# A list scheduler that counts VectorE's time twice where an operation may choose its engine, and durations of products fitted to the trace

## The chip, the cores and the metric

The kernel runs on one core of a Trainium2 chip. The metric is the device time of one execution in microseconds. Before the change it is 1055.45 us (median of 3 runs, 1055.14 to 1056.12).

A core has five engines with a queue of instructions each: PE (TensorE, the matrix products, with PEld for its weight loads), DVE (VectorE), ACT (ScalarE), POOL (GpSimd) and SP (SyncE, which here issues nearly all DMAs). An engine works its queue in order. Between engines there are only semaphores.

## The reference

Three layers follow one another, all in fp32:

```python
# attention: 4 batches, 8 heads, 576 positions of 64, blocks of 64 causal
scores = q @ k.T / 8, masked to block_i >= block_j
attn   = exp(scores - max); attn /= sum + 1e-9
x      = attn @ v                       # 2304 tokens x 512
# first MLP, 512 -> 2048 -> 512, softplus
h = x @ w_in;  g = max(h, 0) + log1p(exp(-|h|));  x = g @ w_out
# second MLP, 512 -> 1536 -> 512, after RMS norm
xn = x / sqrt(mean(x*x) + 1e-6) * rms_g
g = xn @ w_gate;  out = (g * sigmoid(g) * (xn @ w_val)) @ w_out
```

## The kernel before

**Products in two halves.** A fp32 product is made of three passes over operands split into a high and a low part: high x high, high x low, low x high (`PASSES`). So before each product somebody has to make the two parts: a cast (or a scaled copy) writes the high part, a subtraction the low part. For the weights this is `w_unit` (lines 437 to 464): a 128 x 512 piece `wraw` is loaded, ScalarE (L448, L449), VectorE (L458, L452, L456) and GpSimd (L461, an integer addition) make the value `wa`, then the cast `w<-wa` (L327 on ScalarE or L328 on VectorE) and the difference (L337 on VectorE or L338 on GpSimd) fill the two parts of `w`. 68 such pieces pass in the first 660 us.

**Attention.** Work goes by units of one batch, one third of the queries and one pair of heads, 48 in all, and by three query tiles in a unit. For each tile PE makes the scores, VectorE takes their maximum (L627), ScalarE their exponential with its sum (L661), VectorE the reciprocal (L669, L670). Then the rows are scaled by it. The first 12 units (`whole(u)`) take plain fp32 products: the scores `P` are scaled in place (`s_turn`, L703 GpSimd, L704 VectorE or L705 ScalarE), PE transposes them against `ones` (L716), a copy brings them back (`pt`, L722 or L723), and PE multiplies by v. The other 36 units write a high part `pst` in fp16 (`s_split`, L681 GpSimd, L682 VectorE or L683 ScalarE), VectorE the low part (L686), and a DMA transposes both (`pt<-pst`, L693).

**First MLP.** Six blocks of 384 tokens. Its first 9 of 16 slices of the hidden layer (`g1`, products `x,w`; `g2`, products `g,w`) run while attention goes on: each block follows the units that it needs, so that PE always has some wide products to put between the small ones of attention. The other 7 slices follow from some 380 us on, with the weights of the second MLP being prepared beside them.

**Second MLP.** From 660 us to the end PE alone is busy, with nothing left to prepare.

**Who sets the order.** Nothing of this is in program order. Every operation is first entered in a `Plan` with an engine, a duration, a key (roughly its due time) and what it reads and writes. `Plan.schedule` then runs a model of the engines and picks, engine by engine, the ready operation with the lowest key. An operation with `alt` has two or three engines to choose from: in `arrive` it takes the one on which it would end first, by the time at which that engine is free, the durations of the ready operations ahead of it there, and its own duration times `WEIGHT` (line 74). `Plan.emit` repeats this 12 times with keys moved towards the latest start times, keeps the order with the earliest modelled end, and writes the instructions in that order. PE's model has a clock: it runs at half speed unless the tick before it held enough columns (`cols`). Durations come from small functions: `t_mm` for one pass of a product of n columns, `t_mm16` for the columns themselves. `t_mm` also sets the keys of the MLP steps (`step`, `step2`).

Of the kernel before, what the change touches and what calls it, by code (L numbers as in the profile page):

```python
# [68 lines left out]
class Plan:  # L69
# [1 line left out]


    TICK = 10.24 / 3
    WEIGHT = {"ACT": 1, "DVE": 1, "POOL": 1}
    LAT = {"PE": 0.2, "ACT": 0.14, "DVE": 0.2, "POOL": 0.08, "SP": 0.0}
    LAT_DVE = {"DVE": 0.13, "POOL": 0.25}

# [67 lines left out]
    def schedule(self, key):  # L145
# [12 lines left out]
        def arrive(i):  # L158
            if i in self.alts:
                best = None  # L160
                for c, (e, d, _) in enumerate(self.alts[i]):
                    ahead = sum(took[k] for x, k in ready[e] if x < key[i])
                    t = max(ready_at[i], free[e] + ahead)
                    if self.on_port(i, e):
                        t = max(t, port_free)
                    t += d * self.WEIGHT[e]
                    if best is None or t < best[0]:
# [126 lines left out]


def t_mm(n):
    return max(0.11, (n + 32) / 2400)


def t_mm16(n):  # L300
    return n * 0.4167e-3
# [42 lines left out]
def kernel(  # L344
# [14 lines left out]
    S = kT.shape[3]  # L359
# [9 lines left out]
    NG = 3  # L369
    GQ = 192  # L370
# [103 lines left out]
    vhl = [kp.tile([128, 2, KT, 128], FP16, name=f"vhl{p}") for p in range(NP)]  # L474
# [17 lines left out]
    def aop(*args, **kw):  # L492
        att_ops.append(op(*args, **kw))

    def whole(u):
        return u < 12
# [13 lines left out]
    v_pst = [R_pst.new() for _ in range(NP // 2)]  # L510
    v0 = lambda p: v_pst[p // 2]().rearrange("p j c -> p (j c)").bitcast(FP32)[:, 640 * (p % 2):640 * (p % 2) + 640].rearrange("p (a c) -> p a c", c=128)

    def q_slot(u):
        i = u % (4 if whole(u) else 2)
        if i < 2:
            return ("qf", i), lambda: qf[i]
        t = v_pst[i - 2]
        return (t, "q"), lambda: t().rearrange("p j c -> p (j c)").bitcast(FP32)[:, 1280:1664].rearrange("p (i c) -> p i c", i=NG)
# [64 lines left out]
    def ring_a(u):  # L583
        return R_a0 if u * NG < len(units) * NG // NB else R_a
# [9 lines left out]
    def s_tile(u, ib, key, after):  # L594
        b, g, p = units[u]
        n = 64 * (NG * g + ib + 1)
        chunks = [(0, n)] if n <= 512 else [(0, n // 2), (n // 2, n // 2)]
        d = qbd[u % 2]
        if ib == 0:
            pts[u], part[u] = R_pt.new(), (R_nm.new(), [])  # L600
            if not whole(u):
                psts[u] = R_pst.new()
        nm, done = part[u]
        qr = [("qbd", u % 2, l) for l in range(2)]
        kr = [("khl", p, 0), ("khl", p, 1)]
        if whole(u):
            kt, k = k_cell(p), lambda: k0(p)
            (qc, qt), kr = q_slot(u), [kt]
            qr = [qc]
        bank = []  # L610
        for c0, cn in chunks:
            sp = ring_a(u).new()
            bank.append(sp)

            def qk(sp=sp, c0=c0, cn=cn):
                if whole(u):
                    mm(sp()[:, :cn], qt()[:, ib, :], k()[:, c0:c0 + cn], True, True)
                    return
                for m, (a, c) in enumerate(PASSES):
                    mm(sp()[:, :cn], d[:, a, ib, :], khl[p][:, c, c0:c0 + cn], m == 0, m == 2)  # L620

            if c0 == 0:
                qk_op.append(len(plan.ops))
            aop("PE", max(0.213, 0.006 + cn * 1.667e-3) if whole(u) else 3 * t_mm(cn), key, qk, qr + kr, [sp], after=after, cols=t_mm16((2 if whole(u) else 3) * cn))
        for c, (sp, (c0, cn)) in enumerate(zip(bank, chunks)):
            col = ib + c
            aop("DVE", t_dve(cn), key, lambda sp=sp, col=col, cn=cn: nc.vector.tensor_reduce(nm()[:, col:col + 1], sp()[:, :cn], axis=AX.X, op=ALU.max, negate=True), [sp], [(nm, ib)])  # L627
        if len(chunks) == 2:
            aop("DVE", 0.07, key, lambda: nc.vector.tensor_tensor(nm()[:, ib:ib + 1], nm()[:, ib:ib + 1], nm()[:, ib + 1:ib + 2], ALU.min), [(nm, ib)], [(nm, ib)])
        done.append((ib, n, bank, chunks, key))  # L630
        if whole(u):
            if 0:
                if ib < NG - 1:
                    return
                todo, i0, i1 = done, 0, NG
            else:
                todo, i0, i1 = [done[-1]], ib, ib + 1
            cells = [(nm, i) for i in range(i0, i1)]
            small(("DVE", "POOL"), lambda e: e.tensor_scalar(nm()[:, i0:i1], nm()[:, i0:i1], 0.125, 1.0, ALU.mult, ALU.mult), key, cells, cells)
        else:  # L640
            todo = [done[-1]]
        for x in todo:
            s_exp(u, *x)
        if not 0:
            for x in todo:
                s_norm(u, x[0], x[0] + 1, x[4])
                (s_turn if whole(u) else s_split)(u, x[0], x[1], x[4])
        elif ib == NG - 1:
            s_norm(u, 0, NG, key)
            for x in done:  # L650
                s_split(u, x[0], x[1], x[4])
# [75 lines left out]
    def pv_whole(u, key):  # L727
        b, g, p = units[u]
        pt, o, pitch = pts.pop(u), ring_a(u).new(), 2 + g
        nj = (64 * (NG * g + NG) + 127) // 128  # L730
        pf = lambda: pt().rearrange("p j c -> p (j c)").bitcast(FP32).rearrange("p (x c) -> p x c", c=128)

        def prod():
            for j in range(nj):
                i0 = max(0, 2 * j - NG * g)
                kk = min(128, S - 128 * j)
                for h in range(2):
                    mm(
                        o()[64 * h:64 * h + 64, 64 * i0:GQ],
                        v0(p)[0:kk, j, 64 * h:64 * h + 64],  # L740
                        pf()[0:kk, slice(i0 * pitch + j, (NG - 1) * pitch + j + 1, pitch), 64 * h:64 * h + 64],
                        j == 0,
                        j == nj - 1,
                    )

        n = sum(GQ - 64 * max(0, 2 * j - NG * g) for j in range(nj))
        aop("PE", 2e-3 * n, key, prod, [(pt, i) for i in range(NG)] + [(v_pst[p // 2], p)], [o], cols=t_mm16(2 * n))
        jb, off = divmod(b * S + g * GQ, BLK)
        if jb not in x_b:
            x_b[jb] = R_x.new()  # L750
        x = x_b[jb]
        aop("ACT", t_act(GQ, False), key, lambda: nc.scalar.copy(x()[:, p, 0, off:off + GQ], o()[:, :GQ]), [o], [(x, p, 0)])
        aop("DVE", 0.27, key, lambda: nc.vector.tensor_tensor(x()[:, p, 1, off:off + GQ], o()[:, :GQ], x()[:, p, 0, off:off + GQ].bitcast(FP32), ALU.subtract), [o, (x, p, 0)], [(x, p, 1)])  # L753

    def pv(u, key):
        if whole(u):
            pv_whole(u, key)
            return
        b, g, p = units[u]
        pt, o = pts.pop(u), ring_a(u).new()  # L760
        njm = (64 * (NG * g + NG) + 127) // 128

        def prod():
            for j in range(njm):
                i0 = max(0, 2 * j - NG * g)
                kk = min(128, S - 128 * j)
                for m, (a, c) in enumerate(PASSES):
                    for h in range(2):
                        mm(
                            o()[64 * h:64 * h + 64, 64 * i0:GQ],  # L770
                            vhl[p][0:kk, a, j, 64 * h:64 * h + 64],
                            pt()[0:kk, slice(i0 * PITCH[g] + 2 * j + c, (NG - 1) * PITCH[g] + 2 * j + c + 1, PITCH[g]), 64 * h:64 * h + 64],
                            j == 0 and m == 0,
                            j == njm - 1 and m == 2,
                        )

        aop("PE", sum(3 * (t_mm16(GQ - 64 * max(0, 2 * j - NG * g)) + 0.027) for j in range(njm)), key, prod, [(pt, i) for i in range(NG)] + [("vhl", p, 0), ("vhl", p, 1)], [o], cols=sum(t_mm16(3 * (GQ - 64 * max(0, 2 * j - NG * g))) * min(128, S - 128 * j) / 128 for j in range(njm)))
        jb, off = divmod(b * S + g * GQ, BLK)
        if jb not in x_b:
            x_b[jb] = R_x.new()  # L780
        x = x_b[jb]
        aop("ACT", 0.304, key, lambda: nc.scalar.activation(x()[:, p, 0, off:off + GQ], o()[:, :GQ], ACTF.Copy, scale=dsc[p]), [o, ("dsc", p)], [(x, p, 0)])
        aop("DVE", 0.329, key, lambda: nc.vector.scalar_tensor_tensor(x()[:, p, 1, off:off + GQ], o()[:, :GQ], dsc[p], x()[:, p, 0, off:off + GQ].bitcast(FP32), ALU.mult, ALU.subtract), [o, ("dsc", p), (x, p, 0)], [(x, p, 1)])
# [235 lines left out]
    for s in range(len(steps) + LAG):  # L1019
# [5 lines left out]
        if s >= LAG:  # L1025
            j, f = steps[s - LAG]
# [5 lines left out]
        if s < len(steps) and steps[s][1] == NJ[steps[s][0]] - 1:  # L1032
            j = steps[s][0]
# [33 lines left out]
    for s in range(max(n_b + LAG, place[-1] + 1)):  # L1067
# [3 lines left out]
        if s < n_b:  # L1071
            j, f = steps[s]
            n = order.index(j)
# [3 lines left out]
        if LAG <= s < n_b + LAG:  # L1077
            j, f = steps[s - LAG]
            g2(j, f, f == NJ[j], f == NF1 - 1, key_b(s) + 0.5 * step)
            if f == NF1 - 1:  # L1080
                evac_b(j, key_b(s) + 0.6 * step)
                n = order.index(j) + 1
# [10 lines left out]
    for s in range(len(steps) + LAG):  # L1093
        key = t_2 + s * step2
# [4 lines left out]
        if s >= LAG:  # L1099
            j, f = steps[s - LAG]  # L1100
# [70 lines left out]
```

## Time and profile before

| | |
|---|---|
| median of 3 runs | 1055.45 us |
| the profiled execution | 1055.07 us |
| its span, first to last instruction | 1053.0 us |
| granted clock of TensorE, mean over the span | 0.992 |
| PE busy | 1015.6 us (96% of the span) |
| DVE busy | 710.2 us (67%) |
| ACT busy | 529.4 us (50%) |
| POOL busy | 163.9 us (16%) |
| chain that ended last | PE 56%, DVE 4%, DMA 3%, ACT 1% |

The averages hide that the span has different parts. In the page's 40 slices PE is busy for six to nine tenths in the first seven slices and for nine tenths or more from there to the end but for the last; VectorE is at nine tenths or near it over the first 14 slices and at two to four tenths in the last 15. A share of the whole span says little about any of them, so the rows below are taken stage by stage.

### The profile page before, as it was taken

What the parts mean: (1) busy time and instruction counts of PE and PEld (TensorE: products, weight loads), DVE (VectorE), ACT (ScalarE), POOL (GpSimd) and SP (SyncE); (2) the same over time, 40 slices, a digit from 0 to 9 for tenths busy, and PEclk for the clock granted to TensorE, in tenths of its full rate; (3) what the DMA queues carried; (4) which work ended last, traced back from release to release, by engine and by line L of the source; (5) the groups of instructions that cost most, each with busy time, mean ns of one, the idle gap of its engine ahead of it and who ended that gap; (6) DMA issues with size and microseconds to landing.
All of it is one profiled execution on the core that took longest, in us unless ns stands there. A gap on an engine that the chain in (4) does not pass through costs nothing.

```text
span 1053.0 us, 16902 instructions
## 1 busy us (share of the span) xinstructions
PE 1015.6 (96%) x6136; PEld 944.8 (90%) x6136; DVE 710.2 (67%) x1763; ACT 529.4 (50%) x1245; POOL 163.9 (16%) x225
## 2 busy tenths in 40 slices
PE   6798799999999999999999999999999999999998
PEld 4486689899999999999999999999999999999997
DVE  7989999999989967788879999522422422322222
ACT  6786787685767656777767563211211211211211
POOL 2333211211131003322333333000000000000000
PEclk8999899999999999999999999999999999999999
DMA  7444595785856453654544544300100100000000
GB/s 255 141 165 138 169 220 113 172 220 110 204 133 138 89 116 105 214 192 169 216 165 161 187 136 130 98 1 1 60 1 2 61 1 1 31 1 1 31 1 31
DMA packets 111635, 115.19 MB, mean 109 GB/s; under 512 B 84544, under 2 KB 92352, under 8 KB 110528
## 3 DMA queue, kind: packets, MB, share of 16 engines
q1 hardware_dynamic: 110976, 107.83, 36.3%
q0 software_dynamic: 576, 6.29, 1.6%
q8 instruction: 48, 0.79, 0.3%
q14 instruction: 35, 0.29, 0.1%
HBM read 72.03 MB, written 21.63 MB: 89 GB/s over the span
## 4 chain that ended last, share of the span: by engine, by line
PE 56%; DVE 4%; DMA 3%; ACT 1%; issue 1%; POOL 0%; ACTq 0%; DVEq 0%; POOLq 0%; SPq 0%
PE b L422 56%; DMA pt<-pst 1%; DMA wraw<-in_w2gv_dram 1%; DMA wraw<-in_w_dram 1%; DVE wa L456 0%; DVE g L337 0%; DVE r L891 0%; POOL wa L461 0%; DVE t L836 0%; ACT t L834 0%; DVE y L913 0%; DVE wa L458 0%; DVE y L884 0%; ACT wa L448 0%; ACT t L833 0%
## 5 line engine op out<-in xcount | busy, mean ns | idle before, releaser
L422 PE MATMUL b<-x,w 128*128 128x384 f32 x2880 | 546.1, 339 | 0.2 <-DVE x L753 0.2
L422 PEld LDWEIGHTS b<-x,w 128*128 128x128 f32 x2880 | 505.1, 188 | 11.7 <-issue 1.6
L422 PE MATMUL b<-g,w 128*128 128x384 f32 x1152 | 228.3, 341 | 3.6 <-DVE g L337 2.0
L422 PEld LDWEIGHTS b<-g,w 128*128 128x128 f32 x1152 | 200.9, 189 | 7.9 <-DVE g L337 3.4
L422 PE MATMUL b<-w,g 128*128 128x512 f32 x648 | 160.8, 393 | 0.0
L932 DVE TENSOR_TENSOR t<-b,t 128x384 f32<-128x384 f32 x72 | 39.9, 556 | 165.1 <-ACT t L931 165.1
L422 PEld LDWEIGHTS b<-w,g 128*128 128x128 f32 x648 | 120.6, 188 | 21.7
L461 POOL TENSOR_TENSOR wa<-wa,wraw 128x512 int32<-128x512 int32 x68 | 95.6, 1407 | 214.7 <-DVE wa L456 122.0
L931 ACT ACTIVATE t<-b 128x384 f32<-128x384 f32 x72 | 35.2, 491 | 175.5 <-PE b L422 175.5
L934 ACT CAST g<-t 128x384 fp32r<-128x384 f32 x72 | 36.9, 513 | 147.0 <-DVE t L933 147.0
L661 ACT ACTIVATE P<-b,nm 128x288 f32<-128x288 f32 (+8 forms) x160 | 79.4, 499 | 37.7 <-DVE nm L627 14.2
L933 DVE TENSOR_TENSOR t<-b,t 128x384 f32<-128x384 f32 x72 | 40.0, 556 | 62.3 <-PE b L422 62.3
L627 DVE TENSOR_REDUCE nm<-b 128x1 f32<-128x288 f32 (+8 forms) x160 | 70.0, 446 | 8.4 <-PE b L422 8.0
L422 PE MATMUL b<-khl,qbd 128*128 128x448 f32 (+7 forms) x360 | 69.4, 314 | 5.6 <-ACT P L661 3.3
L686 DVE SCALAR_TENSOR_TENSOR pst<-P,nm,pst 128x128 f16<-128x128 f32 (+4 forms) x108 | 67.7, 635 | 1.8 <-POOL pst L681 1.2
L422 PEld LDWEIGHTS b<-khl,qbd 128*128 128x128 f32 x360 | 57.1, 189 | 9.9 <-ACT P L661 4.8
L448 ACT ACTIVATE wa<-wraw 128x512 f32<-128x512 f32 x68 | 45.7, 673 | 35.6 <-DMA wraw<-in_w_dram 20.2
L327 ACT CAST g<-t 128x384 fp32r<-128x384 f32 x96 | 48.6, 511 | 29.5 <-DVE t L836 23.9
L935 DVE TENSOR_TENSOR g<-t,g 128x384 fp32r<-128x384 f32 x72 | 40.0, 556 | 34.3 <-ACT g L934 34.3
L836 DVE SCALAR_TENSOR_TENSOR t<-b,t 128x384 f32<-128x384 f32 x96 | 52.3, 550 | 15.7 <-ACT t L835 15.7
L337 DVE TENSOR_TENSOR g<-t,g 128x384 fp32r<-128x384 f32 x96 | 56.6, 595 | 8.7 <-ACT g L327 8.2
L833 ACT ACTIVATE t<-b 128x384 f32<-128x384 f32 x96 | 46.5, 487 | 25.6 <-PE b L422 25.2
(91 smaller groups left out, 1007.5 us busy)
## 6 DMA issues: line engine op xcount, KB each, us to landing
wraw<-in_w_dram SPq DMA_DIRECT2D x32, 512.0 KB, 3.7
wraw<-in_w2gv_dram SPq DMA_DIRECT2D x24, 512.0 KB, 3.7
yd<-y SPq DMA_DIRECT2D x12, 768.0 KB, 3.6
y<-yd SPq DMA_DIRECT2D x12, 768.0 KB, 4.4
qf<-in_qP_dram SPq DMA_DIRECT2D x42, 192.0 KB, 3.1
xd<-x SPq DMA_DIRECT2D x4, 1536.0 KB, 7.0
x<-xd POOLq DMA_DIRECT2D x4, 1536.0 KB, 7.2
wraw<-in_w2o_dram SPq DMA_DIRECT2D x12, 512.0 KB, 3.6
```

What stands on the lines that cost most here:

```text
L327: "ACT": ("ACT", t_act(n), lambda: nc.scalar.copy(dst(), src())),
L337: "DVE": ("DVE", t_dve(n), lambda: nc.vector.tensor_tensor(dst(), a(), b(), ALU.subtract)),
L422: nc.tensor.matmul(o, lhsT=l, rhs=r, start=start, stop=stop)
L448: op("ACT", t_act(CW), prio, lambda a=a, hv=halves: nc.scalar.activation(a(), hv()[1].bitcast(FP32), ACTF.Abs), [raw], [a])
L461: op("POOL", t_pool2(CW), prio, lambda a=a, hv=halves: nc.gpsimd.tensor_tensor(a().bitcast(I32), a().bitcast(I32), hv()[0].bitcast(I32), A ...
L627: aop("DVE", t_dve(cn), key, lambda sp=sp, col=col, cn=cn: nc.vector.tensor_reduce(nm()[:, col:col + 1], sp()[:, :cn], axis=AX.X, op=ALU.m ...
L661: aop("ACT", 0.24 + cn * 0.836e-3, key, lambda sp=sp, col=col, c0=c0, cn=cn: nc.scalar.activation(P()[:, c0:c0 + cn], sp()[:, :cn], ACTF.E ...
L686: aop("DVE", t_dve(c, True), key, lambda: nc.vector.scalar_tensor_tensor(lo(), pc(), r(), hi(), ALU.mult, ALU.subtract), [P, (P, "pad"), ( ...
L833: op("ACT", t_act(BLK, False), key - 5, lambda: nc.scalar.activation(e(), h()[:, :BLK], ACTF.Abs), [h], [e])
L836: op("DVE", t_dve(BLK), key - 5, lambda: nc.vector.scalar_tensor_tensor(e(), h()[:, :BLK], 0.0, e(), ALU.max, ALU.add), [h, e], [e])
L933: op("DVE", t_dve(BLK), key + 4, lambda: nc.vector.tensor_tensor(u(), va()[:, :BLK], u(), ALU.mult), [va, u], [u])
L935: op("DVE", t_dve(BLK), key + 4, lambda: nc.vector.tensor_tensor(g()[:, 1], u(), g()[:, 0].bitcast(FP32), ALU.subtract), [u, (g, 0)], [(g, ...
```

## The change

Four things, all in what the scheduler believes; the operations of the kernel, their operands and the engines that they may run on stay as they are.

- `WEIGHT["DVE"]` is 2 instead of 1: where an operation may choose, VectorE's duration counts twice in the comparison. Operations that can only run on VectorE are not touched, nor is the time that they take in the model.
- `t_mm(n)`, the duration of one pass of n columns, is 2.5 ns + 0.4459 ns per column, at least 60 ns, in place of (n + 32) / 2400 us, at least 110 ns. At 384 columns both give 0.173 to 0.174 us; at 128 columns and below it falls from 110 to 60 ns.
- The columns that plain fp32 products count for the clock's model are 4 for each column instead of 2 (scores of the first 12 units, and their product with v).
- The product of `pt` and v is entered with `t_mm` + 6 ns for each pass instead of `t_mm16` + 27 ns.

```diff
-    WEIGHT = {"ACT": 1, "DVE": 1, "POOL": 1}
+    WEIGHT = {"ACT": 1, "DVE": 2, "POOL": 1}
...
 def t_mm(n):
-    return max(0.11, (n + 32) / 2400)
+    return max(0.06, 2.5e-3 + n * 0.4459e-3)
...
-            aop("PE", max(0.213, 0.006 + cn * 1.667e-3) if whole(u) else 3 * t_mm(cn), key, qk, qr + kr, [sp], after=after, cols=t_mm16((2 if whole(u) else 3) * cn))
+            aop("PE", max(0.213, 0.006 + cn * 1.667e-3) if whole(u) else 3 * t_mm(cn), key, qk, qr + kr, [sp], after=after, cols=t_mm16((4 if whole(u) else 3) * cn))
...
-        aop("PE", 2e-3 * n, key, prod, [(pt, i) for i in range(NG)] + [(v_pst[p // 2], p)], [o], cols=t_mm16(2 * n))
+        aop("PE", 2e-3 * n, key, prod, [(pt, i) for i in range(NG)] + [(v_pst[p // 2], p)], [o], cols=t_mm16(4 * n))
...
-        aop("PE", sum(3 * (t_mm16(GQ - 64 * max(0, 2 * j - NG * g)) + 0.027) for j in range(njm)), key, prod,
+        aop("PE", sum(3 * (t_mm(GQ - 64 * max(0, 2 * j - NG * g)) + 0.006) for j in range(njm)), key, prod,
```

Counted over the whole program, these instructions change their engine; all others stay on theirs and only change places:

| operation | before: DVE / ACT / POOL | after: DVE / ACT / POOL |
|---|---|---|
| scale of `P` (L704 / L705 / L703) | 27 / 9 / 0 | 1 / 19 / 16 |
| high part `pst` (L682 / L683 / L681) | 67 / 31 / 10 | 0 / 73 / 35 |
| cast `w<-wa` (L328 / L327) | 60 / 8 / - | 1 / 67 / - |
| difference of `w` (L337 / - / L338) | 59 / - / 9 | 49 / - / 19 |
| difference of `qbd` (L337 / - / L338) | 20 / - / 16 | 14 / - / 22 |
| high part `qbd` (- / L327 / L329) | - / 27 / 9 | - / 22 / 14 |

The order shows it at three places. First GpSimd's queue from the first tiles on, first as before (`P` are the scores that are scaled, `nm` their maxima and sums, `wa` a weight piece):

```order
L658 MEMSET P 128x64 x3
L639 ISA
L639 TENSOR_SCALAR nm<-nm 128x1
L658 MEMSET P 128x64
L461 TENSOR_TENSOR wa<-wa,wraw 128x512
L639 TENSOR_SCALAR nm<-nm 128x1
```

After the change:

```order
L658 MEMSET P 128x64 x2
L703 ISA
L703 TENSOR_SCALAR P<-P,nm 128x64
L703 TENSOR_SCALAR P<-P,nm 128x128
L703 TENSOR_SCALAR P<-P,nm 128x192
L658 MEMSET P 128x64
L703 TENSOR_SCALAR P<-P,nm 128x256
L639 TENSOR_SCALAR nm<-nm 128x1
L658 MEMSET P 128x64
L461 TENSOR_TENSOR wa<-wa,wraw 128x512 x2
L658 MEMSET P 128x64
L703 TENSOR_SCALAR P<-P,nm 128x64
```

The first four scales of `P` now stand on GpSimd, ahead of the weight additions, and the next three right behind two of these. Before, the first four stood on VectorE. Over the program 8 of the 16 scales on GpSimd have an addition L461 as the last longer instruction ahead of them.

Second, PE's queue where the first product of the MLP (`x,w`) joins the first 12 units (`ones,P` are transposes, `pt,pst` the products with v, `raw,qf` and `y,qf` scores), first as before:

```order
L422 MATMUL b_357<-raw,qf_107 128x192
L422 MATMUL b_365<-pt,pst 64x192 x2
L422 MATMUL b_365<-pt,pst 64x64 x2
L716 MATMUL b_380<-ones,P 128x128 x3
L716 MATMUL b_389<-ones,P 128x128 x3
L422 MATMUL b_399<-raw,qf_108 128x256
L716 MATMUL b_409<-ones,P 128x128
L422 MATMUL b_415<-raw,qf_108 128x320
```

After the change:

```order
L422 MATMUL b_348<-raw,qf_107 128x192
L716 MATMUL b_355<-ones,P 128x128 x2
L422 MATMUL b_362<-pt,pst 64x192 x2
L422 MATMUL b_362<-pt,pst 64x64 x2
L422 MATMUL b_371<-x,w 128x384 x3
L716 MATMUL b_380<-ones,P 128x128 x3
L422 MATMUL b_384<-x,w 128x384 x3
L422 MATMUL b_397<-y,qf_107 128x448
L716 MATMUL b_406<-ones,P 128x128 x3
L422 MATMUL b_414<-raw,qf_108 128x256
```

After the change two groups of three wide products and the scores of a later unit stand between the two groups of transposes that followed each other before; the first `x,w` product is 14 rows earlier in the queue. From there to the end of attention PE's queue holds the same products at nearly the same places.

Third, VectorE's queue in the middle of attention, at the low part of the keys of the third batch (`khl_95`), first as before:

```order
L337 TENSOR_TENSOR g<-t,g 128x384
L682 TENSOR_SCALAR pst<-P,nm 128x5x128
L669 TENSOR_SCALAR nm<-nm 128x1
L627 TENSOR_REDUCE nm<-b_2136 128x1
L686 SCALAR_TENSOR_TENSOR pst<-P,nm,pst 128x5x128
L670 RECIPROCAL nm<-nm 128x1
L627 TENSOR_REDUCE nm<-b_2157 128x1
L669 TENSOR_SCALAR nm<-nm 128x1
L552 SCALAR_TENSOR_TENSOR khl_95<-raw,khl_95 128x576
```

After the change:

```order
L337 TENSOR_TENSOR g<-t,g 128x384
L670 RECIPROCAL nm<-nm 128x1
L627 TENSOR_REDUCE nm<-b_2098 128x1
L686 SCALAR_TENSOR_TENSOR pst<-P,nm,pst 128x4x128
L629 TENSOR_TENSOR nm<-nm 128x1
L686 SCALAR_TENSOR_TENSOR pst<-P,nm,pst 128x4x128
L783 SCALAR_TENSOR_TENSOR x<-b_2014,dsc_104,x 128x192
L663 TENSOR_TENSOR nm<-nm 128x1
L552 SCALAR_TENSOR_TENSOR khl_95<-raw,khl_95 128x576
```

The high parts (L682) are gone from this queue; VectorE makes only the low parts (L686), and waits for a high part that another engine has made.

## Rows read from the trace of the kernel before

**Rows 1.** Four stages: stretch, length, busy of PE PEld DVE ACT POOL, clock, DMA

```profile
0.00:200.00 200.00, 169.83 (x1099) 140.72 (x1100) 180.68 (x580) 143.53 (x376) 52.02 (x95) 0.96 0.61 172
200.00:380.00 180.00, 177.93 (x1413) 167.42 (x1411) 163.72 (x509) 123.67 (x342) 27.57 (x70) 1.00 0.68 150
380.00:660.00 280.00, 278.76 (x1583) 272.13 (x1584) 242.61 (x453) 187.21 (x377) 84.31 (x61) 1.00 0.49 164
660.00:1053.00 393.00, 389.10 (x2046) 364.50 (x2044) 123.16 (x224) 75.02 (x151) 0.00 (x0) 1.00 0.06 20
```

**Rows 2.** Whom PE waited for: us in total, times, longest

```profile
PE b L716 <- DVE P L704: 6.7, 8, 2.3
PE b L422 <- DMA qf<-in_qP_dram: 4.3, 1, 4.3
PE b L422 <- ACT P L661: 3.9, 7, 1.8
PE b L716 <- ACT P L705: 3.6, 5, 1.5
...
PE b L422 <- DVE g L337: 2.0, 5, 0.5
PE b L422 <- ACT pt L722: 1.7, 2, 1.2
PE b L422 <- ACT g L327: 1.6, 1, 1.6
PE b L422 <- DVE nm L639: 1.5, 1, 1.5
```

**Rows 3.** Two stretches at half the granted clock, columns as in rows 1

```profile
110.50:117.30 6.80, 6.37 (x31) 4.54 (x31) 6.80 (x26) 4.42 (x13) 2.23 (x3) 0.50 0.49 127
127.55:130.95 3.40, 3.40 (x13) 3.40 (x12) 3.40 (x13) 2.14 (x8) 1.16 (x2) 0.50 0.90 278
```

**Rows 4.** VectorE groups: operation, count, busy us, mean ns, idle before it

```profile
L458 DVE TENSOR_SCALAR wa<-wa 128x512 f32<-128x512 f32 x68 | 39.4, 580 | 8.1 <-ACT wa L448 7.7
L682 DVE TENSOR_SCALAR pst<-P,nm 128x384 f16<-128x384 f32 (+4 forms) x67 | 34.7, 518 | 1.7 <-DMA pt<-pst 1.1
...
L328 DVE CAST w<-wa 128x512 fp32r<-128x512 f32 x60 | 26.5, 442 | 4.9 <-POOL wa L461 4.8
...
L704 DVE TENSOR_SCALAR P<-P,nm 128x64 f32<-128x64 f32 (+8 forms) x27 | 11.9, 445 | 0.3
```

**Rows 5.** VectorE, first 200 us: busy of line 682, then of line 328

```profile
0.00:200.00 200.00, 10.51 (x19) 0.96 0.61 172
...
0.00:200.00 200.00, 7.47 (x18) 0.96 0.61 172
```

**Rows 6.** ScalarE groups, columns as in rows 4

```profile
L661 ACT ACTIVATE P<-b,nm 128x288 f32<-128x288 f32 (+8 forms) x160 | 79.4, 499 | 37.7 <-DVE nm L627 14.2 <-DVE nm L639 10.3 <-DVE nm L669 4.7
...
L683 ACT ACTIVATE pst<-P,nm 128x384 f16<-128x384 f32 (+3 forms) x31 | 17.5, 572 | 8.4 <-issue 4.5 <-DVE nm L670 2.4 <-DMA pt<-pst 0.6
...
L705 ACT ACTIVATE P<-P,nm 128x384 f32<-128x384 f32 (+6 forms) x9 | 5.4, 601 | 1.6 <-DVE nm L670 1.5
L327 ACT CAST w<-wa 128x512 fp32r<-128x512 f32 x8 | 5.0, 621 | 3.0 <-POOL wa L461 3.0
```

**Rows 7.** GpSimd groups, columns as in rows 4

```profile
L461 POOL TENSOR_TENSOR wa<-wa,wraw 128x512 int32<-128x512 int32 x68 | 95.6, 1407 | 214.7 <-DVE wa L456 122.0 <-ACT wa L448 21.6 <-ACT t L835 16.3
...
L338 POOL TENSOR_TENSOR w<-wa,w 128x512 fp32r<-128x512 f32 x9 | 13.6, 1512 | 22.3 <-ACT w L327 11.3 <-DVE w L328 11.0
...
L681 POOL TENSOR_SCALAR pst<-P,nm 128x128 f16<-128x128 f32 (+3 forms) x10 | 7.2, 718 | 17.4 <-DVE nm L670 15.0 <-DVE dsc L569 1.7 <-DVE am L565 0.5
```

**Rows 8.** Line 458 on VectorE: duration min/median/max in ns

```profile
L458 DVE TENSOR_SCALAR wa<-wa x68: 403/422/1584, 11.1 to 653.2; 128x512 f32<-128x512 f32 x68
```

**Rows 9.** Timeline from 13.4 us: start, length, instruction

```profile
13.44 1.29 POOL L461 TENSOR_TENSOR wa<-wa,wraw 128x512 int32<-128x512 int32 x1 [1.00 <-ACT wa L448]
...
13.61 1.40 DVE L458 TENSOR_SCALAR wa<-wa 128x512 f32<-128x512 f32 x1
```

More of the change, by code (lines that the diff above doesn't have):

```diff
@@ L775, in prod @@
                         )
-        aop("PE", sum(3 * (t_mm16(GQ - 64 * max(0, 2 * j - NG * g)) + 0.027) for j in range(njm)), key, prod, [(pt, i) for i in range(NG)] + [("vhl", p, 0), ("vhl", p, 1)], [o], cols=sum(t_mm16(3 * (GQ - 64 * max(0, 2 * j - NG * g))) * min(128, S - 128 * j) / 128 for j in range(njm)))
+        aop("PE", sum(3 * (t_mm(GQ - 64 * max(0, 2 * j - NG * g)) + 0.006) for j in range(njm)), key, prod, [(pt, i) for i in range(NG)] + [("vhl", p, 0), ("vhl", p, 1)], [o], cols=sum(t_mm16(3 * (GQ - 64 * max(0, 2 * j - NG * g))) * min(128, S - 128 * j) / 128 for j in range(njm)))
         jb, off = divmod(b * S + g * GQ, BLK)
```

## The prediction

> **What bounds the kernel now.** I read the stages first, because the shares of the whole span mix unlike parts. From 380 us to the end PE is busy for all but 5.1 of 673 us at the full granted clock, whatever VectorE does [rows 1]; nothing that the choice of an engine changes can be won there, though 42 of the 60 casts `w<-wa` of VectorE lie behind the first 200 us [rows 4, 5]. From 200 to 380 us PE idles for 2.1 us. In the first 200 us it idles for 30.2 us, VectorE is busy for 180.7 (90%), ScalarE for 143.5 (72%), GpSimd for 52.0 (26%), and the mean clock is 0.96 [rows 1]. So the change is decided in the first 200 us.
>
> Second, the waits of PE. Of these 30.2 us, 10.2 end with VectorE (the scale of `P` 6.7, `g` 2.0, `nm` 1.5), 10.8 with ScalarE (the exponentials 3.9, the scale of `P` 3.6, `pt` 1.7, `g` 1.6), 4.3 is the first load, and 4.9 are smaller ones (30.2 - 10.2 - 10.8 - 4.3; a little of `g` falls later) [rows 1, 2]. The waits on ScalarE are in part VectorE's: the exponentials were held up for 29.2 us by VectorE's maxima, their scaling and other work on `nm` (14.2 + 10.3 + 4.7) [rows 6]. Third, the clock: it stands at half, the lower of its two levels (1.2 of 2.4 GHz), for 6.8 us from 110.5 us on and for 3.4 us from 127.6 us on [rows 3]. PE had gaps before the first of them. A third such stretch of 6.8 us lies in the start-up and will stay.
>
> **What it removes.** The 67 high parts `pst`, 26 of the 27 scales of `P` and 59 of the 60 casts leave VectorE. Of the high parts 19 lie in the first 200 us, of the casts 18 [rows 5], of the scales all 27. That is 10.5 + 7.5 us [rows 5] and 26/27 x 11.9 = 11.5 us [rows 4], together 29.5 us: VectorE goes from 180.7 to about 151 us (76%). The few differences that also leave it are not counted.
>
> **What it adds.** ScalarE gets 10 scales of `P` at 601 ns = 6.0 us, 18 casts at 621 ns = 11.2 us, and of the 19 high parts those that GpSimd doesn't take. Over the program ScalarE gains 42 and GpSimd 25 of 67; in that proportion 12 at 572 ns = 6.9 us [rows 6]. ScalarE goes from 143.5 to about 168 us (84%). GpSimd gets 16 scales of `P`, which it never ran before: bounded by a high part on GpSimd (718 ns) [rows 7] from above and VectorE's own 445 ns [rows 4] from below; I take 718, since it is the same engine and a like operation. With 7 high parts that is 23 x 0.718 = 16.5 us, and GpSimd goes from 52 to some 69 us (34%); its 10 more differences of `w` at 1512 ns [rows 7] reach past 200 us. PE's products stay, at nearly the same places; the new durations of products only move keys, and I cost them at nothing, covered by PE's in-order queue, which holds the same work (if that cover fails, it shows as waits of PE, the third rival).
>
> **The sum**, against the profiled execution's 1055.07 us, 0.4 below the median:
> - Waits that end with VectorE: 10.2 us, of which I take 8.5 as gone. The operations that it hands over are the very ones that PE waited for, and what is left on it queues behind less. What is late next is the same scale on ScalarE or GpSimd. Bounds: 0 and 10.2.
> - Waits that end with ScalarE: 10.8 us, of which I take 6. They get shorter where ScalarE itself stood behind VectorE, longer where 24 us more work stand ahead. Bounds: -6 (half as long again, if its queue decides) and 10.8.
> - Smaller waits: half of 4.9, 2.5. Bounds 0 and 4.9.
> - The clock: 6.8 + 3.4 us at half rate cost at most half of that, 5.1 us of full-rate work. I take half, 2.5, as the gaps before the first stretch go in part. Bounds: -3.4 (one more such stretch of 6.8 us) and 5.1.
> - Against it: 16 scales that take 718 - 445 = 273 ns longer on GpSimd, 4.4 us, half of it in front of PE: -2.2. Bounds 0 and -14 (third rival).
>
> 8.5 + 6 + 2.5 + 2.5 - 2.2 = 17.3, so 1055.07 - 17.3 = 1037.8, and I say 1038. A second count agrees: the busiest engine of the first 200 us was VectorE at 90%, and becomes ScalarE at 168 us. At the same 90% the stretch takes 186 us, 14 less; the clock's 2.5 come on top.
>
> **A rule that speaks against it.** At 13.44 us GpSimd starts an addition of 1.29 us; at 13.61 VectorE starts L458, which takes 1.40 us in place of its median 0.42 [rows 8, 9]. Over 68 of these the mean stands at 580 ns [rows 4], so they lose 68 x 0.158 = 10.7 us beside 163.9 us of busy GpSimd, 0.065 us for each. For 16.5 us more on GpSimd that is 1.1 us on VectorE, which the sum leaves out.
> The Trainium skill, SBUF — State Buffer, section "Who interferes with whom", says that GpSimd and VectorE share one pair of ports, and that whichever starts first holds it for its whole instruction while the other fully blocks. The two rows at 13.4 us agree. By the rule in full, if each of the 23 new GpSimd instructions held up VectorE for its length, VectorE would lose 16.5 us, more than half of its relief, the first term would shrink from 8.5 to some 3.7 us, and the sum would give 1042.6 instead of 1037.8; by the row's price it stays at 1038.
>
> **Rivals.**
> *Bigger: nearly all gaps close (chance 0.16).* For it: with VectorE at 76% and ScalarE at 84%, no engine beside PE is full in the first 200 us, and wide `x,w` products stand earlier between the transposes. Against: the start-up chain of the first tiles is a chain whatever the load. Time: 10.2 + 10.8 + 4.9 + 5.1 = 31.0, 1024.
> *ScalarE takes VectorE's place (0.10).* For it: it gets 24 us more, and it does the exponentials that head each tile's chain. Its occupancy in the first 200 us need not rise to 90%, since it also waits for VectorE and for loads; at 84% its 168 us take 200 us, as now. Against: now it has 28% free, and loses much of its waiting with VectorE's relief. Time: 1055, no change. That the new durations alone are what acts, and do nothing, would give the same.
> *GpSimd becomes what the transposes wait for (0.09): slower.* Place: the first 100 us, `ones,P` on PE behind scales on GpSimd. 8 of the 16 scales have an addition L461 as the last longer instruction ahead of them, which takes 1407 ns [rows 7]. If half of these 8 x 1.41 = 11.3 us and the 4.4 us of longer scales reach PE, 7.8 us come, the 6.7 us on `P` [rows 2] stay, the waits on ScalarE that follow them grow by 6, and longer gaps cost one more half-clock stretch, 3.4. Left of the gain are 2.5 of smaller waits and 0.8 x 3.5 = 2.8 of VectorE's others, and the clock's 2.5 don't come. 7.8 + 6 + 3.4 - 5.3 = +11.9, at the worst 1067; with half of that, 1061. It decides once waits on GpSimd pass some 17 us, the gain of the forecast. Against: GpSimd is busy for only 26% of this stage now, and a wait reaches PE only when no wide product stands ready before the transposes.
>
> **How the numbers follow.** Chances: forecast 0.65 (1029 to 1047 by the terms' middle bounds), bigger 0.16 (near 1024), no change 0.10, slower 0.09. The range of 8 in 10 goes from 1023 to 1053: below it is the full closing of all gaps, above it most of the two rivals that bring nothing or less. A measurement of this kernel can tell a change of about 0.2% (2.1 us) from none. Faster by more than that: 0.65 + 0.16 and a fifth of the no-change case, 0.83; within it: 0.07; slower: the third rival and what ScalarE's case leaves over, 0.10.
>
> **What would show it.** Right: in the first 200 us of the changed kernel (some 182 long for the same products) PE idles for less than 17 us, VectorE falls below 80%, ScalarE rises above 80%, and the waits of PE on `P` by VectorE are nearly gone, without waits on `P` by GpSimd of more than 4 us. From 380 us of the old count on, all is as before. The half-clock stretches after 100 us are gone or shorter. Wrong: waits of `ones,P` on GpSimd or ScalarE above 10 us (the rivals), VectorE still at 90%, or a stage after 200 us with more than 5 us of idle PE, which would mean that the moved casts and differences of weights arrive late.

## The result and the profile after

The changed kernel takes 1040.22 us (median of 4 runs, 1039.91 to 1040.66) against 1055.78 us for the kernel before on the same chip: a ratio of 0.9852 with an interval of 0.9835 to 0.9869, some 15.6 us less. The forecast was 1038. Its profiled execution spans 1038.3 us, 14.7 less than before, at a mean granted clock of 0.998 (before 0.992).

The stages, with the columns of [rows 1], and one more stretch that holds as many products as the first 200 us of before, of nearly the same kinds (1097 against 1099; 226 of them `x,w` against 222):

```profile
0.00:200.00 200.00, 180.03 (x1250) 153.27 (x1251) 177.36 (x560) 169.85 (x448) 80.36 (x138) 0.99 0.69 194
200.00:380.00 180.00, 177.19 (x1369) 167.17 (x1368) 145.33 (x426) 137.85 (x364) 42.69 (x86) 1.00 0.62 133
380.00:660.00 280.00, 279.07 (x1556) 271.53 (x1556) 229.62 (x399) 201.10 (x399) 90.98 (x67) 1.00 0.48 164
660.00:1038.00 378.00, 373.66 (x1965) 349.96 (x1964) 115.49 (x209) 71.31 (x143) 0.00 (x0) 1.00 0.05 18
```

```profile
0.00:183.00 183.00, 163.55 (x1097) 138.02 (x1098) 162.80 (x505) 157.59 (x412) 74.42 (x127) 0.99 0.66 185
```

What took 200 us takes 183. This stretch alone gains some 17 us; what follows gives about 2 us back and gains nothing. In it PE idles for 19.5 us instead of 30.2. VectorE is busy for 162.8 us instead of 180.7, which is still 89% of the shorter time; ScalarE has gone from 143.5 to 157.6 (86%), GpSimd from 52.0 to 74.4 (41%).

Whom PE waits for now, columns as in [rows 2]:

```profile
PE b L422 <- DMA qf<-in_qP_dram: 4.4, 1, 4.4
PE b L716 <- ACT P L705: 3.7, 1, 3.7
PE b L422 <- ACT pt L722: 3.0, 4, 1.4
PE b L422 <- DMA pt<-pst: 2.9, 5, 0.9
PE b L422 <- DVE g L337: 1.9, 3, 1.2
PE b L716 <- DVE P L704: 1.3, 1, 1.3
PE b L422 <- ACT P L661: 1.2, 3, 0.6
PE b L716 <- ACT P L661: 1.0, 2, 0.6
PE b L422 <- DVE nm L669: 0.8, 1, 0.8
...
PE b L422 <- DVE t L836: 0.5, 2, 0.3
```

Against [rows 2] the wait for `P` on VectorE has gone from 6.7 to 1.3 us and `nm` L639 from 1.5 to nothing; no wait for GpSimd has come. The waits that end with ScalarE have hardly fallen, from 10.8 to 8.9 (3.7 + 3.0 + 1.2 + 1.0), and now hold one single wait of 3.7. With the smaller rows of the same view added, and in the first 200 us (183 after) alone, the waits that end with VectorE go from 13.9 to 4.8 us, those that end with ScalarE from 11.0 to 9.3, those on DMAs stay at 4.9. So nearly all of the idle time that is gone had ended with VectorE.

Half the granted clock is left for one stretch of 3.4 us in the start-up, where before it stood so for 6.8 us; the two of [rows 3] are gone, and between 100 and 150 us the clock is full. The start-up's stretch before:

```profile
14.88:21.71 6.83, 6.14 (x20) 3.77 (x22) 6.83 (x27) 3.91 (x12) 2.52 (x6) 0.50 0.81 275
```

After the change:

```profile
100.00:150.00 50.00, 46.82 (x355) 42.42 (x354) 47.31 (x159) 43.22 (x120) 18.84 (x34) 1.00 0.81 205
16.95:20.38 3.43, 3.41 (x11) 2.68 (x12) 3.11 (x15) 3.31 (x11) 1.07 (x4) 0.50 0.95 311
```

This is one execution. By the mean granted clock of each, the four executions of the changed kernel lose 2.1 to 6.2 us of their span to the clock (span x (1 - mean clock)), this one the least, and 25 executions of the kernel before 3.2 to 12.7.

The groups that moved, over the whole span, on VectorE, ScalarE and GpSimd in turn [rows 4, 6, 7]:

```profile
L458 DVE TENSOR_SCALAR wa<-wa 128x512 f32<-128x512 f32 x68 | 38.6, 570 | 11.7 <-ACT wa L448 11.4
...
L704 DVE TENSOR_SCALAR P<-P,nm 128x256 f32<-128x256 f32 x1 | 1.4, 1370 | 0.0
L328 DVE CAST w<-wa 128x512 fp32r<-128x512 f32 x1 | 0.4, 429 | 0.6 <-POOL wa L461 0.6
```

```profile
L661 ACT ACTIVATE P<-b,nm 128x288 f32<-128x288 f32 (+8 forms) x160 | 80.1, 502 | 16.3 <-DVE nm L639 4.5 <-DVE nm L627 2.9 <-DVE nm L669 2.8
L683 ACT ACTIVATE pst<-P,nm 128x256 f16<-128x256 f32 (+4 forms) x73 | 44.6, 614 | 14.4 <-DVE nm L670 8.1 <-DMA pt<-pst 1.4 <-DVE dsc L569 1.3
L327 ACT CAST w<-wa 128x512 fp32r<-128x512 f32 x67 | 41.6, 622 | 12.8 <-POOL wa L461 12.6
...
L705 ACT ACTIVATE P<-P,nm 128x320 f32<-128x320 f32 (+8 forms) x19 | 11.9, 631 | 1.6 <-DVE nm L669 0.9 <-DVE nm L639 0.6
```

```profile
L461 POOL TENSOR_TENSOR wa<-wa,wraw 128x512 int32<-128x512 int32 x68 | 95.2, 1401 | 204.0 <-DVE wa L456 119.1 <-ACT wraw L449 20.4 <-ACT t L833 13.5
...
L681 POOL TENSOR_SCALAR pst<-P,nm 128x128 f16<-128x128 f32 (+4 forms) x35 | 23.8, 680 | 51.6 <-DVE nm L670 15.6 <-ACT g L327 9.8 <-ACT P L661 7.9
L703 POOL TENSOR_SCALAR P<-P,nm 128x64 f32<-128x64 f32 (+7 forms) x16 | 9.1, 570 | 12.2 <-DVE nm L669 8.0 <-ACT x L752 2.5 <-DVE nm L670 1.3
```

The exponentials L661 are held up by VectorE's maxima and sums for 10.2 us where it was 29.2 [rows 6].

### The profile page after: what moved, and what is told of

It reads as the page before. It is cut to its first block, busy times and chain, and to the rows that moved or that the text cites. A ratio compares the mean times of both kernels' runs of the same rounds, so it can differ in the third digit from the quotient of the medians.

```text
span 1038.3 us, 16885 instructions
## 1 busy us (share of the span) xinstructions
PE 1009.9 (97%) x6136; PEld 941.9 (91%) x6136; DVE 667.8 (64%) x1592; ACT 580.1 (56%) x1352; POOL 214.0 (21%) x289
## 4 chain that ended last, share of the span: by engine, by line
PE 73%; DVE 9%; ACT 8%; DMA 7%; issue 2%; POOL 1%; SPq 0%; POOLq 0%; ACTq 0%; DVEq 0%
PE b L422 73%; DMA pt<-pst 4%; DMA wraw<-in_w_dram 2%; ACT P L661 1%; POOL wa L461 1%; ACT wa L448 1%; DVE wa L456 1%; DVE g L337 1%; ACT w L327 1%; DVE nm L627 1%; DVE wa L458 1%; DVE pst L686 1%; DVE t L836 1%; ACT t L834 1%; ACT P L705 1%
## 5 line engine op out<-in xcount | busy, mean ns | idle before, releaser
L461 POOL TENSOR_TENSOR wa<-wa,wraw 128x512 int32<-128x512 int32 x68 | 95.2, 1401 | 204.0 <-DVE wa L456 119.1
L661 ACT ACTIVATE P<-b,nm 128x288 f32<-128x288 f32 (+8 forms) x160 | 80.1, 502 | 16.3 <-DVE nm L639 4.5
L686 DVE SCALAR_TENSOR_TENSOR pst<-P,nm,pst 128x128 f16<-128x128 f32 (+4 forms) x108 | 68.3, 638 | 9.1 <-ACT pst L683 6.7
L337 DVE TENSOR_TENSOR g<-t,g 128x384 fp32r<-128x384 f32 x96 | 60.5, 632 | 11.4 <-ACT g L327 10.9
L836 DVE SCALAR_TENSOR_TENSOR t<-b,t 128x384 f32<-128x384 f32 x96 | 52.6, 551 | 21.4 <-ACT t L835 21.0
L935 DVE TENSOR_TENSOR g<-t,g 128x384 fp32r<-128x384 f32 x72 | 42.9, 597 | 35.4 <-ACT g L934 35.4
L327 ACT CAST g<-t 128x384 fp32r<-128x384 f32 x96 | 49.2, 516 | 19.9 <-DVE t L836 16.8
```

Of the source, the lines that this page charges most:

```text
L327: "ACT": ("ACT", t_act(n), lambda: nc.scalar.copy(dst(), src())),
L337: "DVE": ("DVE", t_dve(n), lambda: nc.vector.tensor_tensor(dst(), a(), b(), ALU.subtract)),
L461: op("POOL", t_pool2(CW), prio, lambda a=a, hv=halves: nc.gpsimd.tensor_tensor(a().bitcast(I32), a().bitcast(I32), hv()[0].bitcast(I32), A ...
L661: aop("ACT", 0.24 + cn * 0.836e-3, key, lambda sp=sp, col=col, c0=c0, cn=cn: nc.scalar.activation(P()[:, c0:c0 + cn], sp()[:, :cn], ACTF.E ...
L686: aop("DVE", t_dve(c, True), key, lambda: nc.vector.scalar_tensor_tensor(lo(), pc(), r(), hi(), ALU.mult, ALU.subtract), [P, (P, "pad"), ( ...
L836: op("DVE", t_dve(BLK), key - 5, lambda: nc.vector.scalar_tensor_tensor(e(), h()[:, :BLK], 0.0, e(), ALU.max, ALU.add), [h, e], [e])
```

## The experiments

The theory to be tested (A): VectorE, full in the first 200 us, sets the pace there, and the gain is its relief. Its rivals: the new durations of products make the gain by moving wide products forward (B); or any new order from this scheduler moves the time by as much (C). After the first four runs A was narrowed to two loads in series (`P`, then `pst`), and after the first eight a further theory was set beside it (D): there is no one load whose removal does it, all that is taken off VectorE counts together. Every run decides all its choices anew and so has a new order as well; none changes one operation's engine and leaves the rest in place.

The measured numbers of all runs; the ratio is from all executions, the columns behind the interval from the one that was profiled. "Idle" is the span less PE's busy time, "clock" the span times (1 - mean granted clock, given to three digits, so to half a us), "rest" the span less both:

| run | ratio to before | interval | DVE busy in first 200 us | span | idle | clock | rest |
|---|---|---|---|---|---|---|---|
| before | 1 | | 180.7 | 1053.0 | 37.4 | 8.4 | 1007.2 |
| after | 0.9852 | 0.9835-0.9869 | 177.4 | 1038.3 | 28.4 | 2.1 | 1007.8 |
| weight alone | 0.9916 | 0.9883-0.9949 | 170.9 | 1046.3 | 33.8 | 5.2 | 1007.3 |
| products alone | 1.0027 | 1.0012-1.0042 | 184.5 | 1055.6 | 39.5 | 10.6 | 1005.5 |
| weight for `P` | 0.9974 | 0.9958-0.9990 | 180.7 | 1051.1 | 34.5 | 7.4 | 1009.2 |
| weight but for `P` | 0.9994 | 0.9977-1.0012 | 169.6 | 1057.5 | 36.7 | 13.7 | 1007.1 |
| before, reshuffled | 0.9993 | 0.9980-1.0006 | 181.5 | 1054.4 | 38.8 | 8.4 | 1007.2 |
| after, reshuffled | 0.9865 | 0.9844-0.9887 | 174.9 | 1039.9 | 31.0 | 4.2 | 1004.7 |
| weight 3 | 0.9933 | 0.9911-0.9955 | 169.1 | 1047.2 | 32.2 | 9.4 | 1005.6 |
| weight 1.5 | 1.0048 | 1.0032-1.0065 | 179.1 | 1057.4 | 37.2 | 15.9 | 1004.3 |
| weight for `P`, `pst` | 0.9950 | 0.9932-0.9968 | 174.0 | 1046.7 | 32.1 | 8.4 | 1006.2 |
| `P` not on GpSimd | 0.9933 | 0.9914-0.9952 | 174.0 | 1046.0 | 29.7 | 10.5 | 1005.8 |
| three weights | 0.9853 | 0.9838-0.9867 | 176.4 | 1037.5 | 24.9 | 7.3 | 1005.3 |
| differences on DVE | 0.9903 | 0.9887-0.9919 | 174.6 | 1045.2 | 30.0 | 7.3 | 1007.9 |

**The weight alone, and the products alone.**

```diff
 (on the kernel before)
-    WEIGHT = {"ACT": 1, "DVE": 1, "POOL": 1}
+    WEIGHT = {"ACT": 1, "DVE": 2, "POOL": 1}
```

> The kernel before with VectorE's weight 2 alone; durations and columns of products as before. Theory A (relief of VectorE in the first 106 us makes the gain): about 1040 us, 13 to 18 less than before. Theory B (the new durations of products put wide products earlier among the transposes, and that makes the gain): within 3 us of before, some 1054. Theory C (any new order of this scheduler moves the time by as much, by luck): anything from 1035 to 1060, unrelated to VectorE's load.

```diff
 (on the changed kernel)
-    WEIGHT = {"ACT": 1, "DVE": 2, "POOL": 1}
+    WEIGHT = {"ACT": 1, "DVE": 1, "POOL": 1}
```

> The changed kernel with VectorE's weight back at 1: new durations and columns of products alone. Theory A: within 3 us of before, with VectorE at 90% of the first 200 us. Theory B: about 1040. Theory C: anything from 1035 to 1060.

Measured: 0.9916, about 9 us less, and 1.0027, about 3 us more. B falls: alone the new durations cost time. A is not met in full either: the weight alone gives 9 of 15.6 us. The two together give more than their sum (-9 and +3), so they need each other. One half of how is in the waits of PE in the run with the weight alone:

```profile
PE b L716 <- ACT P L705: 8.4, 12, 1.5
...
PE b L716 <- POOL P L703: 2.7, 2, 1.9
```

In its first 200 us the waits that end with VectorE are down to 2.2 us, but those that end with ScalarE are up at 14.9 (11.0 before) and 2.7 have come on GpSimd; the scales of `P` that moved there make up the rise. In the changed kernel these are 9.3 and nothing. So the second and the third rival of the prediction act in part where the weight stands alone; the new durations, with which wide products stand between the transposes and 16 scales instead of 8 go to GpSimd, come with most of that gone. The other half is seen in the first product `x,w` of PE and what follows. Counted are PE's products with `x`, in the first 106 us and from there to 200 (the columns are the stretch, its length, PE's busy time with the number of products, the granted clock, the DMA share and GB/s). Before:

```profile
0.00:106.00 106.00, 20.54 (x84) 0.97 0.53 174
106.00:200.00 94.00, 30.43 (x138) 0.95 0.70 170
```

The changed kernel, the same view:

```profile
0.00:106.00 106.00, 23.52 (x108) 0.98 0.56 183
106.00:200.00 94.00, 35.10 (x173) 1.00 0.83 206
```

The weight alone:

```profile
0.00:106.00 106.00, 19.45 (x84) 0.95 0.53 174
106.00:200.00 94.00, 33.73 (x156) 1.00 0.80 188
```

The products alone:

```profile
0.00:106.00 106.00, 23.00 (x96) 0.94 0.52 174
106.00:200.00 94.00, 28.31 (x132) 0.96 0.72 169
```

The products alone bring 12 more wide products into the first 106 us and lose 6 again by 200. The waits of PE in that run say where:

```profile
PE b L716 <- ACT P L705: 5.5, 2, 4.2
PE b L422 <- DVE t L836: 4.6, 4, 2.2
PE b L422 <- DMA qf<-in_qP_dram: 4.4, 1, 4.4
PE b L422 <- ACT P L661: 3.3, 4, 1.5
PE b L422 <- DVE nm L627: 3.2, 1, 3.2
```

Wide products that come earlier ask VectorE earlier for their softplus (`t`, L836), and VectorE is full: 4.6 us on L836, 1.3 before and 0.5 in the changed kernel.

**The weight for the scale of `P` alone, and for all but it.**

```diff
+        plan.twice.add(len(plan.ops))    # first run; the second: plan.once
         aop2([alts[e] for e in ('POOL', 'ACT', 'DVE')], key, [P, (nm, "r", ib)], [P])
...
-                    t += d * self.WEIGHT[e]
+                    t += d * (self.WEIGHT[e] if i in self.twice else 1)    # first run
+                    t += d * (1 if i in self.once else self.WEIGHT[e])     # second run
```

> The changed kernel with the weight 2 only for the scale of P in the first 12 units (37 choices); everything else compares with weight 1. Theory A with the direct wait on P as its core: PE waited 6.7 us for this scale on VectorE, and it takes 11.5 us off VectorE in the first 100 us: 6 to 11 us less than before, 1044 to 1049. If the casts are as important, only 3 to 6 less. Theory B: about 1040. Theory C: no relation.

> The changed kernel with the weight 2 for all choices except the scale of P. Theory A: the rest of the gain, 5 to 9 us less than before, 1046 to 1050, and PE still waits several us for P on VectorE; together with the run of P alone it makes up about 15 us. Theory B: about 1040. Theory C: no relation.

Measured: 0.9974 and 0.9994, some 3 us less and no change that can be told from none (there are 36 of these choices, not 37). A expected 15 us from the two together and gets 3. The scales of `P` alone leave PE waiting 5.9 us for L836 again (its line is one further on here):

```profile
PE b L422 <- DVE t L837: 5.9, 4, 3.1
PE b L717 <- ACT P L705: 5.6, 4, 3.6
```

All but `P` has VectorE busy for only 169.6 us of the first 200 and still gains nothing. A said that PE would still wait several us for `P` on VectorE, and that is a miss: 24 of the 36 scales stay there, and PE waits for them for 1.5 us (6.7 before). Its largest waits are 4.7 us on ScalarE's exponentials and 4.6 on `pt<-pst`. Its profiled execution was the slowest of ten (1059.30 against a median of 1055.20), so its row in the table has some 4 us of span too much, and its clock's loss of 13.7 us is the top of 7.4 to 13.7. Why this run gains nothing stays open; VectorE's busy time alone does not foretell the time.

**Luck of the order.**

```diff
-            a = 0.15
+            a = 0.14
```

> The kernel before with the step of the keys between the 12 passes of the scheduler at 0.14 instead of 0.15: another order with no new belief. It measures luck. Theory A (two loads of VectorE in series in the first 200 us, P and pst, must both go): within 4 us of before, VectorE at 90%. Theory C (luck of the order): it may move by 10 us or more either way.

> The changed kernel with the same 0.14. Theory A: 1036 to 1045, that is at least two thirds of the gain stays, since VectorE is relieved just as far. Theory C: it may fall back to 1050 or more.

Measured: 0.9993 and 0.9865. One other order under the same beliefs, tried once for each kernel, moves the time by less than 2 us. C falls as the cause of 15 us, as far as two orders can tell; differences of 1 to 2 us between these runs mean little.

**Other weights.**

```diff
-    WEIGHT = {"ACT": 1, "DVE": 2, "POOL": 1}
+    WEIGHT = {"ACT": 1, "DVE": 3, "POOL": 1}      # and 1.5
```

> The changed kernel with VectorE's weight 3: 67 of 68 differences of weights go to GpSimd at 1.5 us each (19 in the changed kernel). Theory A with GpSimd as the next limit: 2 to 8 us slower than the changed kernel (1042 to 1048), PE waits for weights or for P on GpSimd. If VectorE's load alone matters: as fast or up to 5 us faster. Theory C: no relation.

> The changed kernel with VectorE's weight 1.5: 48 of 108 high parts pst and 57 of 68 casts stay on VectorE, 20 of 37 scales of P. Theory A: between the run with the products alone (+3 us) and the changed kernel (-16 us), some 1046 to 1054. Theory C: no relation.

Measured: 0.9933 and 1.0048. Weight 3 is 8.5 us slower than 2, a little past what A said: GpSimd is busy for 292 us of the span (214 at weight 2), but PE hardly waits for it; it waits for ScalarE's `pt` instead (4.3 + 2.7 us), and the clock loses 9.4 us. Weight 1.5 was to lie between and is the slowest of all: 48 high parts and 57 casts on VectorE, 8.3 us of waits for L836, 15.9 us of clock. D was set up after that miss: by it each load that stays lets the wide products run into VectorE.

**The scale of `P` and the high part `pst` alone.**

> The changed kernel with the weight 2 only for the scale of P and the high part pst; casts and differences of weights compare with weight 1, so that 55 of 68 casts stay on VectorE. Theory A (P in the first 100 us and pst in the second, two loads of VectorE in series): at least two thirds of the gain, 1040 to 1046. Theory D (the casts of weights in the first 100 us are needed as well, since every operation taken off VectorE counts while it is full): 1047 to 1053.

The same edit as for `P`, at both choices. Measured: 0.9950, 5.3 us less. Theory A (two loads in series) falls here, and D's range holds: with 55 of 68 casts still on VectorE, PE waits 4.9 us for L836 (two lines further on here):

```profile
PE b L718 <- ACT P L706: 5.5, 4, 3.3
PE b L422 <- ACT P L661: 4.9, 5, 1.3
PE b L422 <- DVE t L838: 4.9, 4, 2.1
```

**GpSimd out of the choice for `P`; all differences of weights on VectorE.**

```diff
-        aop2([alts[e] for e in ('POOL', 'ACT', 'DVE')], key, [P, (nm, "r", ib)], [P])
+        aop2([alts[e] for e in ('ACT', 'DVE')], key, [P, (nm, "r", ib)], [P])
```

> The changed kernel with GpSimd taken out of the choice for the scale of P; 17 of 36 go back to VectorE at twice the price, 19 stay on ScalarE. If GpSimd's part in it is worth its longer instructions: 3 to 8 us slower than the changed kernel, 1043 to 1048, with VectorE fuller in the first 100 us. If these scales on GpSimd only cost (port, longer chain): 1 to 4 us faster.

```diff
-            op2(differences(..., ("DVE", "POOL")), prio, [a, (w, 0, c)], [(w, 1, c)])
+            op2(differences(..., ("DVE",)), prio, [a, (w, 0, c)], [(w, 1, c)])
```

> The changed kernel with all 68 differences of weights on VectorE (49 in the changed kernel), so that GpSimd has 19 instructions of 1.5 us less. If GpSimd's occupancy by long instructions holds anything up: 1 to 4 us faster than the changed kernel. If VectorE's load decides: 1 to 5 us slower.

Measured: 0.9933, 8 us slower than the changed kernel, and 0.9903, 5 us slower. GpSimd's part in both is worth its longer instructions, which is the third rival of the prediction turned round. The second run is less clean than its edit: 11 scales of `P` instead of 16 stand on GpSimd in it, and PE waits 5.3 us for L836 (2.7 + 2.6).

**Three weights.**

```diff
-    WEIGHT = {"ACT": 1, "DVE": 2, "POOL": 1}
+    WEIGHT = {"ACT": 1.15, "DVE": 2.5, "POOL": 1.3}
```

> The changed kernel with weights 1.15 for ScalarE, 2.5 for VectorE and 1.3 for GpSimd: the same relief of VectorE, and less on GpSimd (25 high parts pst in place of 35, 9 high parts qbd in place of 14). ScalarE was busy for 47.9 of 50 us between 50 and 100 us in the changed kernel, so a better spread may gain 1 to 4 us more, 1036 to 1039; if the spread makes no difference, as the changed kernel within 2 us.

Measured: 0.9853, as the changed kernel (1040.12 us). The least idle of all, 24.9 us, and 7.3 us of clock against 2.1. No version that ran beats the changed kernel.

## Why the prediction came out right

*The time and its place.* 1040.2 against 1038, 15.6 us gained of 17.3, and all of it in the first 200 us; from 380 us on PE idles as little as before. VectorE's weight, not the new durations by themselves, carries it: with the new durations in both, weight 2 in place of 1 takes 1.0027 to 0.9852. That it acts by what PE waited for on VectorE fits the waits (13.9 to 4.8 us); no run shows it apart from the new order that the weight brings as well.

*The terms, however, were right only in sum, and that is luck.* The rest in the table is 1004 to 1009 us in all 14 kernels, so the span of each is its idle plus its clock's loss plus nearly a constant. By that the 14.7 us of the two profiled spans are 9.0 of idle (37.4 to 28.4) and 6.3 of clock (8.4 to 2.1), less 0.6. The sum had 8.5 + 6 + 2.5 - 2.2 = 14.8 for the waits and 2.5 for the clock. The term of the waits that end with ScalarE was mis-sized: 6 taken, 1.9 measured (10.8 to 8.9). ScalarE did wait less for VectorE before its exponentials (29.2 to 10.2 us), but PE now waits for the scales on ScalarE, 10 more than before, and for its copies. The smaller waits fell by 1.6 of the 2.5 taken (from 4.9 to what is left of 19.5 without the load, VectorE's three groups and 8.6 of ScalarE's in that stretch, 3.3). The 2.2 us against it for longer scales on GpSimd did not show as a wait.

The clock's term was mis-sized the other way: in these two executions 6.3, past its upper bound of 5.1, because it left out the start-up's stretch, which it said would stay and which halved from 6.8 to 3.4 us. Over all executions the difference is smaller, 7.7 us lost on the mean of 25 before and 3.9 on the mean of four after. And idle and clock are not independent: an execution of the changed kernel that lost 6.2 us to the clock spans 1038.6 us, against 1038.3 for the one that lost 2.1. So how the 15.6 us divide between the two is known only roughly.

*Waits that end with VectorE* went as said: the three groups of [rows 2] from 10.2 to 3.2 us (1.3 + 1.9 + 0), 7.0 gone of the 8.5 taken.

*VectorE's relief* was to be 29.5 us and a fall to 76% busy, and is 17.9 us (180.7 to 162.8 for the same products) at 89%. That sign in the list of what would show it was wrong, and so was another: PE idles for 19.5 us of its stretch, not for less than 17. The step that failed is to take durations off a busy time. The durations of VectorE's instructions in these stretches add up to 224.1 us before and 197.0 after, 27.1 less; but instructions that follow one another overlap in the trace, 43.1 us of the sum before and 34.1 after, so the engine's busy time falls by less than the durations taken out. ScalarE shows the same: 26.9 us more of durations, 14.1 us more of busy time. On VectorE contention comes on top: the same instruction in the same stretch, first before (to 200 us), then after (to 183):

```profile
L337 DVE TENSOR_TENSOR g<-t,g 128x384 fp32r<-128x384 f32 x18 | 9.8, 551 | 0.6 <-ACT g L327 0.6
...
L629 DVE TENSOR_TENSOR nm<-nm 128x1 f32<-128x1 f32 x8 | 1.2, 146 | 0.0
```

```profile
L337 DVE TENSOR_TENSOR g<-t,g 128x384 fp32r<-128x384 f32 x18 | 11.3, 631 | 1.1 <-ACT g L327 0.9
...
L629 DVE TENSOR_TENSOR nm<-nm 128x1 f32<-128x1 f32 x8 | 3.6, 446 | 0.0
```

*The rule that spoke against it.* These two groups alone are 3.9 us longer. Operations that left VectorE took their own delays along, so all must be counted: VectorE instructions that take over 60 ns more than the median of their like are 20 before and 28 after in these stretches, 11.0 and 14.2 us over it in all, and every one of them runs beside a GpSimd instruction. That is some 3 us more, so the row's price of 1.1 us was too low. The longest of the small ones ends with the addition on GpSimd that started before it:

```profile
62.62 1.51 POOL L461 TENSOR_TENSOR wa<-wa,wraw 128x512 int32<-128x512 int32 x1
62.88 1.26 DVE L629 TENSOR_TENSOR nm<-nm 128x1 f32<-128x1 f32 x1
```

The Trainium skill, SBUF — State Buffer, section "Who interferes with whom", has the one that issues second blocked for the whole of the other's instruction, where VectorE needs the shared pair of ports; for a VectorE instruction with two inputs in SBUF it says that it contends with a GpSimd instruction that reads SBUF. L337 and L629 have two such inputs, and the two rows agree. Had each of the 23 new GpSimd instructions held VectorE for its whole length, it would have been 16.5 us; the measured price lies between the two.

*ScalarE as the next engine that paces* (second rival): 157.6 us of 183 (86%), where that rival had 168 of 200; VectorE stayed the fullest engine. In part it came true: half of PE's idle time now ends with ScalarE (9.3 of 19.5 us). *GpSimd in front of the transposes* (third rival): no wait of PE for it, 0.57 us for each scale instead of the 0.718 taken; without GpSimd in the choice for `P` the kernel is 8 us slower. *Products' durations at nothing*: they cost 3 us alone, and are worth some 6 beside the weight, which gets 9 us without them and 15.6 with them; that term was put at nothing on the ground that PE's queue holds the same work, and its order turned out to matter. The prediction named the earlier wide products only as a sign for the bigger gain; they are part of the gain.

What stays open: whether the clock falls only because of PE's gaps, or could be held up by other means, was not tried; runs with like idle differ by 3 us of clock (`P` not on GpSimd 29.7 and 10.5, differences on VectorE 30.0 and 7.3), which is no more than executions of one kernel differ by. Nor is it shown why the single effects are so far from adding up; the waits for L836 and for the scales on ScalarE name parts of it. D describes this and does not explain it.

## What to carry to other kernels

Where several engines share a stage, look in that stage alone for the engine on which the bounding one's waits end; the busy share does not tell (89% after, with the gain; 85% with all but `P` moved, and none). Price a scheduler's choice for what stands behind it in the queue, not for its own duration: doubling VectorE's cost in the choice gave 0.8%, and 1.5% with fitted durations, with no operation changed. Here a relief in part gained little or nothing (weight 1.5 +0.5%, one or two of the groups 0 to -0.5%), and in three of these four runs PE waited 4.9 to 8.3 us for L836, with VectorE still full. Do not take the durations of removed instructions off an engine's busy time where its instructions overlap. Split a time into idle of the bounding engine, loss of its clock and a rest, over several executions: it shows that the terms of a good sum may be wrong one by one.

## What was not expected of the hardware

The clock's loss varies from 2.1 to 15.9 us between the profiled executions of kernels that do the same work, about as much as the idle time does (24.9 to 39.5), and from 3.2 to 12.7 us between executions of the one kernel before. A 128x1 operation on VectorE (L629) took, among 16 in the changed kernel, from 142 to 1265 ns:

```profile
L629 DVE TENSOR_TENSOR nm<-nm x16: 142/156/1265, 47.2 to 354.2; 128x1 f32<-128x1 f32 x16
```

Its median is 156 (147 before, where the longest took 482); some of these smallest instructions now stand still until a GpSimd instruction that runs beside them ends, as in the two rows at 62.6 us above.
